# Two 256-token tiles of a unit's first chunks in one PSUM bank, stepped at every second attention item

## Chip, cores and metric

One core of a Trainium2 chip runs the whole kernel. The metric is device time in microseconds (us) of one execution.

## What is computed

Windowed attention with four sink tokens, a dense feed-forward layer with a mish-like gate, and a mixture of four dense experts, each on the output of the one before:

```python
scores = where(is_sink | in_window, q @ k.T / sqrt(D), -1e9)   # B,H,S,D = 2,8,768,64; 4 sinks, window 128
x = softmax(scores) @ v                                        # -> 1536 tokens x 512
h = x @ w_in                                                   # 512 x 2048
x = (h * tanh(log1p(exp(h)))) @ w_out                          # 2048 x 512
p = domain_probs / (domain_probs.sum(-1, keepdims=True) + 1e-9)
out = sum(p[:, e:e+1] * (maximum(x @ w1[e], 0) @ w2[e]) for e in range(4))   # F = 1024
```

## The kernel before

Attention is cut into 24 **items**: for each of two batch entries and three blocks of 256 queries, one item per pair of heads (four pairs). So items 0 to 3 make x for tokens 0 to 255, items 4 to 7 for tokens 256 to 511, items 8 to 15 for tokens 512 to 1023, and items 16 to 23 for the rest. An item computes four score tiles (L231), masks and takes row maxima on VectorE (L234), exponentiates on ScalarE (L238), normalises on GpSimd (L252, L255), transposes on TensorE (L264), multiplies with v (L277, L283), and splits the result into a high and a low part, `xh` (L184) and `xl` (L185, VectorE), since each matrix product of the later layers is three products of such parts (`TERMS`).

The feed-forward layers are cut into **units** of 512 hidden columns: four of the mish layer (unit 0 is the first), then eight of the experts. A unit goes over the tokens in **chunks**, 512 tokens each, except that unit 0 starts with two chunks of 256, because their tokens are ready early. `layer1` makes four hidden tiles (f = 0 to 3) of a chunk, each from 12 matmuls (L477) into one PSUM tile `h`, and then applies `mish`: ScalarE L549 to L552 and L554, VectorE L553, L555 and L556, then the split into `gh` (ScalarE L89) and `gl` (GpSimd L97). L549 is the first to read `h` and L556 the last. `layer2` makes four output tiles (d = 0 to 3) from the four hidden ones, 12 matmuls each (L504) into a PSUM tile `o`, which ScalarE copies to `acc` (L510) in unit 0.

`stream` is a generator that hands out these tiles one **step** at a time: for every chunk, its layer 1 mixed with layer 2 of the chunk before. While attention runs, `banded` takes one step after each item from item 5 on (`LAG`), 19 in all, then nine more that finish the fourth chunk, and `rest` does the other units. The 19 steps are the four of chunk 0, the eight of chunk 1 and seven of the eight of chunk 2; chunk 3 is all in the nine. Beside the steps, `run(w, 1)` converts weights from 64-bit words, after items 0 to 3 and those in `PARK`; this is VectorE's `cv_` work (L117 to L124).

During attention the PSUM pools are small: `x.psum(first, 1, 1)` gives one `h` bank, one `o` bank, and a mish buffer `r` in SBUF. So the 12 matmuls of the next hidden tile can start only when L556 of the tile before has read the bank. After the loop, `first.close()` gives these pools and attention's back, `x.psum(ctx, 3, 3, 2)` makes three `h`, three `o` and two `r` banks in their place, and `x.weights(1)` loads the second unit's weights, parked in DRAM, into SBUF that the closed pools held. The order of every engine's queue comes from a scheduler at compile time: it issues ready instructions by program order, so that steps, items and weight conversion are interleaved.

Of the kernel before, what the change touches and what calls it, by code (L numbers as in the profile page):

```python
# [9 lines left out]
F32 = mybir.dt.float32  # L10
F32R = mybir.dt.float32r
# [6 lines left out]
P = 128  # L18
# [7 lines left out]
QW = 2 * P  # L26
STAGE = 1024
AHEAD = 2
LAG = 5
WARM = 12  # L30
PARK = (8, 10, 12, 14, 16, 18)

class Ctx:
# [3 lines left out]
class Ring:  # L37
# [5 lines left out]
    def next(self):  # L43
        self.n += 1
        return self.tiles[(self.n - 1) % len(self.tiles)]
# [39 lines left out]
def copy(c, eng, out, src):  # L85
    if eng is c.nc.gpsimd:
        eng.tensor_scalar(out, src, 1.0, 0.0, ALU.mult, ALU.add)  # L87
    elif eng is c.nc.scalar:
        eng.activation(out, src, AF.Copy)  # L89
    else:  # L90
        eng.tensor_copy(out, src)


def split(c, hi, lo, src, eng_hi, eng_lo):

    copy(c, eng_hi, hi, src)
    eng_lo.tensor_tensor(lo, src, hi.bitcast(F32), ALU.subtract)  # L97
# [67 lines left out]
def banded_masks(c):  # L165

    nc = c.nc
    rel, sink, diag, prev = c.parts
    m0, m1, m2 = c.masks
    nc.vector.tensor_scalar(sink, sink, c.ns, None, ALU.is_ge)  # L170
    nc.vector.scalar_tensor_tensor(diag, rel, c.win, diag, ALU.is_ge, ALU.add)
    nc.vector.scalar_tensor_tensor(m0[:, 0:P], diag, -BIG, sink, ALU.mult, ALU.mult)
    nc.vector.tensor_scalar(prev, rel, float(P), c.win, ALU.add, ALU.is_ge)
    nc.vector.scalar_tensor_tensor(m1[:, 0:P], prev, -BIG, sink, ALU.mult, ALU.mult)
    for m, at, x in ((m1, P, diag), (m2, 0, prev), (m2, P, sink[:, 0:SINKS]), (m2, SEG, diag)):
        nc.gpsimd.tensor_scalar(m[:, at:at + x.shape[1]], x, -BIG, 0.0, ALU.mult, ALU.add)
# [11 lines left out]
def attention_pools(c, ctx):  # L188
    nc = c.nc
    a = Ctx()  # L190
    a.qk = ctx.enter_context(c.tc.tile_pool(name="a_qk", bufs=4))
    v = c.acc[:, 8:12].rearrange("p a w -> p (a w)")
    a.v = Ring([v[:, 3 * P * n:3 * P * (n + 1)].rearrange("p (n d) -> p n d", n=3) for n in range(5)])
    a.p = ctx.enter_context(c.tc.tile_pool(name="a_p", bufs=3))
    a.st = v[0:4 * SINKS, 15 * P:16 * P]
    a.sm = ctx.enter_context(c.tc.tile_pool(name="a_sm", bufs=3))
    a.ps = ctx.enter_context(c.tc.tile_pool(name="a_ps", bufs=3, space=PSUM))
    a.tr = ctx.enter_context(c.tc.tile_pool(name="a_tr", bufs=2, space=PSUM))
    a.pv = ctx.enter_context(c.tc.tile_pool(name="a_pv", bufs=1, space=PSUM))
    a.vsk = c.vsk  # L200
    return a
# [164 lines left out]
TERMS = ((0, 0), (1, 0), (0, 1))  # L366
# [11 lines left out]
class Experts:  # L378
# [86 lines left out]
    def layer1(self, n, t0, cw, g):  # L465
        c, nc = self.c, self.c.nc
        kind, e, _, _ = self.units[n]
        NF, KT, n1 = self.NF, self.KT, self.n1
        x = (c.xh, c.xl)
        cols = slice(t0, t0 + cw)  # L470
        wis = self.w[n][0]
        for f in range(NF):
            h = self.pa.tile([P, self.CW], F32, tag="h", name="h")[:, 0:cw]
            fs = slice(f * P, (f + 1) * P)
            for k in range(KT):
                for t, (sw, sx) in enumerate(TERMS):
                    nc.tensor.matmul(  # L477
                        h, lhsT=wis[sw][:, k, fs], rhs=x[sx][:, k, cols],
                        start=k == 0 and t == 0, stop=k == KT - 1 and t == 2,
                    )  # L480
            gh = self.gp.tile([P, self.CW], F32R, tag="gh", name="gh")[:, 0:cw]
            gl = self.gp.tile([P, self.CW], F32R, tag="gl", name="gl")[:, 0:cw]
            if kind == 0:
                self.mish(n, gh, gl, h)
            else:
                nc.scalar.activation(gh, h, AF.Relu)  # L486
                nc.vector.scalar_tensor_tensor(gl, h, 0.0, gh.bitcast(F32), ALU.max, ALU.subtract)  # L487
            g.append((gh, gl))
            yield

    def layer2(self, n, t0, cw, g):
        c, nc = self.c, self.c.nc
        kind, e, _, _ = self.units[n]
        NF, KT, n1 = self.NF, self.KT, self.n1
        cols = slice(t0, t0 + cw)
        wos = self.w[n][1]
        if kind == 0:
            accv = self.acc.rearrange("p (ch d) w -> p ch d w", d=KT)
            for d in range(KT):
                o = self.pb.tile([P, cw], F32, tag="o", name="o")  # L500
                ds = slice(d * P, (d + 1) * P)
                for f in range(NF):
                    for t, (sw, sx) in enumerate(TERMS):
                        nc.tensor.matmul(  # L504
                            o, lhsT=wos[sw][:, f, ds], rhs=g[f][sx],
                            start=f == 0 and t == 0, stop=f == NF - 1 and t == 2,
                        )
                y = accv[:, t0 // c.DM, d, t0 % c.DM:t0 % c.DM + cw]
                if n == 0:
                    nc.scalar.activation(y, o, AF.Copy)  # L510
                else:
                    nc.vector.tensor_tensor(y, y, o, ALU.add)
                if n == n1 - 1:
                    split(c, c.xh[:, d, cols], c.xl[:, d, cols], y, nc.scalar, nc.vector)
                yield
            return
        last = n == len(self.units) - 1
        for d in range(cw // P):
            tt = t0 // P + d
            pcol = c.pn[:, tt, e:e + 1]  # L520
            ds = slice(d * P, (d + 1) * P)
            nw = 2 if last and tt == c.T // P - 1 else 1
            for q in range(nw):
                ms = slice(q * c.DM // nw, (q + 1) * c.DM // nw)
                o = self.pb.tile([P, c.DM], F32, tag="o", name="o")[:, ms]
                for f in range(NF):
                    for t, (sw, sx) in enumerate(TERMS):
                        nc.tensor.matmul(  # L528
                            o, lhsT=g[f][sx][:, ds], rhs=wos[sw][:, f, ms],
                            start=f == 0 and t == 0, stop=f == NF - 1 and t == 2,  # L530
                        )
                y = self.acc[:, tt, ms]
                if n == n1:
                    nc.scalar.activation(y, o, AF.Copy, scale=pcol)
                else:
                    nc.vector.scalar_tensor_tensor(y, o, pcol, y, ALU.mult, ALU.add)  # L536
                if last:
                    nc.sync.dma_start(out=c.out[tt * P:(tt + 1) * P, ms], in_=y)
            yield
# [20 lines left out]
def run(gen, n=None):  # L560

    while n is None or n > 0:
        if next(gen, run) is run:
            return
        n = None if n is None else n - 1


def banded(c, ctx, raws):

    tc = c.tc  # L570
    banded_masks(c)
    first = ExitStack()
    x = Experts(c, ctx)
    w = x.weights(0)
    x.psum(first, 1, 1)
    a = attention_pools(c, first)
    steps = x.stream([(0, 0, QW), (0, QW, QW)] + [(0, t0, x.CW) for t0 in range(2 * QW, c.T, x.CW)] + later(c, x, 1))
    dram = ctx.enter_context(tc.tile_pool(name="park", bufs=1, space=bass.MemoryType.DRAM))
    w = chain(w, x.park(dram, 1, "wi"), x.park(dram, 1, "wo"), x.park(dram, 2, "wi"))
    items = c.items  # L580
    raws = dict(enumerate(raws))
    preps = {}
    done = 0
    for m, it in enumerate(items):
        while done <= min(m + AHEAD, len(items) - 1):
            raw = raws.pop(done) if done in raws else load_item(c, *items[done], pool=a.qk)
            preps[done] = raw, attention_values(c, a, *items[done])
            done += 1
        attention_item(c, a, *it, preps.pop(m))
        if m < 4 or m in PARK:  # L590
            run(w, 1)
        if m >= LAG:
            run(steps, 1)
        if m == 0:
            normalize_probs(c)
    first.close()
    x.wpool[1] = ctx.enter_context(tc.tile_pool(name="m_w1", bufs=1))
    x.psum(ctx, 3, 3, 2)
    run(x.weights(1))
    run(steps, 4 * (x.NF + 4) - 4 - (len(items) - LAG))  # L600
    rest(c, x, steps, 1)


# [30 lines left out]
def swa_mish_experts_kernel(ctx: ExitStack, tc: tile.TileContext, qk, v, vsink, n_sink, window, w_in, w_out, probs, w1,  # L634
# [30 lines left out]
    with tc.tile_pool(name="warm", bufs=1, space=PSUM) as wp:  # L665
        o = wp.tile([P, P], F32, name="warm")
        for _ in range(WARM):
            nc.tensor.matmul(o, lhsT=c.ident, rhs=c.ident, start=True, stop=True)
# [73 lines left out]
```

## Time and profile before

| quantity | value |
|---|---|
| runs | 929.54, 937.5, 939.44 us (median 937.5) |
| profiled execution | 931.33 us, of which the profile's span is 929.5 us |
| busy share of the span | TensorE (PE) 97%, its weight loads (PEld) 79%, VectorE (DVE) 46%, ScalarE (ACT) 37%, GpSimd (POOL) 28% |
| mean granted TensorE clock | 0.988 of full speed |
| chain of work that ended last | TensorE 86%, VectorE 10% |

TensorE's busy time counts an instruction from its start to a modelled end, and matmuls overlap; twelve matmuls of 512 columns that are each shown with 0.39 us take 2.72 us together. So in the attention stage a busy share near one does not say that the engine is full; the chain of waits says more.

### The profile page before, as it was taken

Reading aid. Unit: us, or ns where it says so; the run is one execution under the profiler, and the core shown is the slowest. Engines: PE = TensorE matmul, PEld = TensorE weight load, DVE = VectorE, ACT = ScalarE, POOL = GpSimd, SP = SyncE. Lnnn points to the kernel's source line nnn. Section 1 sums busy time; section 2 is a strip of 40 time slices with the busy share of each in tenths; the row PEclk is TensorE's granted clock in tenths of the full one; section 3 lists DMA queues with packets and bytes.
Section 4 is the critical chain, followed back from the end, with each engine's and each line's share of the span. In section 5 each row is a group of like instructions: output and inputs, shape, how many; then the busy total and the mean of one; then the engine's idle time right before and its main releaser. Section 6 shows DMA issues by size and latency. Waiting matters only on the chain.

```text
span 929.5 us, 11138 instructions
## 1 busy us (share of the span) xinstructions
PE 905.6 (97%) x4292; PEld 730.6 (79%) x4292; DVE 424.6 (46%) x770; ACT 347.7 (37%) x745; POOL 263.7 (28%) x217
## 2 busy tenths in 40 slices
PE   6999999799999999999999999999999999999997
PEld 4566767688888888888888888888888888888886
DVE  6999995247698555641112222222222222222222
ACT  4788875487767767722221111111111111111110
POOL 4586663122222434520220220221122112200000
PEclk8999999989999999999999999999999999999999
DMA  7757752062123011001110110110110010000012
GB/s 234 249 189 242 251 215 80 17 255 91 46 90 136 1 46 46 23 23 46 46 40 7 45 46 1 46 46 0 46 46 24 23 45 1 1 1 1 11 46 83
DMA packets 33790, 67.03 MB, mean 72 GB/s; under 512 B 4144, under 2 KB 12592, under 8 KB 33728
## 3 DMA queue, kind: packets, MB, share of 16 engines
q1 hardware_dynamic: 33728, 66.23, 21.1%
q8 instruction: 36, 0.59, 0.3%
q14 instruction: 26, 0.21, 0.1%
HBM read 51.54 MB, written 9.44 MB: 66 GB/s over the span
## 4 chain that ended last, share of the span: by engine, by line
PE 86%; DVE 10%; ACT 1%; DMA 1%; issue 0%; POOL 0%; DVEq 0%; ACTq 0%
PE h L477 42%; PE o L528 28%; PE o L504 14%; DVE pr L234 2%; DVE cv_h L119 1%; DVE cv_a L123 1%; PE pv L277 1%; DVE cv_a L117 1%; DVE cv_r L122 1%; DMA stage<-in_moe_w_in_dram 1%; PE sc L231 1%; PE tp L264 1%; DVE cv_a L121 1%; DVE xl L185 1%; DVE cv_a L118 0%
## 5 line engine op out<-in xcount | busy, mean ns | idle before, releaser
L477 PE MATMUL h<-xh,wih 128*128 128x512 f32 (+1 forms) x592 | 229.2, 387 | 0.3 <-DVE w L556 0.3
L477 PE MATMUL h<-xh,wil 128*128 128x512 f32 (+1 forms) x592 | 227.8, 385 | 0.0
L477 PE MATMUL h<-xl,wih 128*128 128x512 f32 (+1 forms) x592 | 226.8, 385 | 0.0
L486 ACT ACTIVATE gh<-h 128x512 fp32r<-128x512 f32 x96 | 57.4, 598 | 410.1 <-PE h L477 245.2
L487 DVE SCALAR_TENSOR_TENSOR gl<-h,gh 128x512 fp32r<-128x512 f32 x96 | 66.4, 691 | 208.1 <-ACT gh L486 207.9
L528 PE MATMUL o<-wol,gh 128*128 128x512 f32 (+1 forms) x388 | 150.1, 387 | 0.0
L528 PE MATMUL o<-woh,gh 128*128 128x512 f32 (+1 forms) x388 | 150.1, 387 | 0.0
L528 PE MATMUL o<-woh,gl 128*128 128x512 f32 (+1 forms) x388 | 149.9, 387 | 0.0
L536 DVE SCALAR_TENSOR_TENSOR acc<-o,pn,acc 128x512 f32<-128x512 f32 (+1 forms) x85 | 63.3, 745 | 176.2 <-PE o L528 176.2
L477 PEld LDWEIGHTS h<-xh,wih 128*128 128x128 f32 x592 | 111.8, 189 | 24.5 <-DVE cv_a L117 0.7
L477 PEld LDWEIGHTS h<-xl,wih 128*128 128x128 f32 x592 | 111.5, 189 | 22.6 <-issue 0.5
L477 PEld LDWEIGHTS h<-xh,wil 128*128 128x128 f32 x592 | 111.7, 189 | 22.3 <-DVE wil L124 0.3
L97 POOL TENSOR_TENSOR gl<-w,gh 128x512 fp32r<-128x512 f32 (+1 forms) x52 | 68.2, 1312 | 168.0 <-ACT gh L89 167.8
L504 PE MATMUL o<-gh,woh 128*128 128x512 f32 (+1 forms) x208 | 79.4, 382 | 5.4 <-ACT gh L89 5.4
L528 PEld LDWEIGHTS o<-wol,gh 128*128 128x128 f32 x388 | 72.9, 188 | 14.9
L528 PEld LDWEIGHTS o<-woh,gh 128*128 128x128 f32 x388 | 72.9, 188 | 14.9
L528 PEld LDWEIGHTS o<-woh,gl 128*128 128x128 f32 x388 | 72.8, 188 | 14.7
L504 PE MATMUL o<-gh,wol 128*128 128x512 f32 (+1 forms) x208 | 78.2, 376 | 0.0
L504 PE MATMUL o<-gl,woh 128*128 128x512 f32 (+1 forms) x208 | 77.4, 379 | 0.0
L87 POOL TENSOR_SCALAR wih<-stage 128x1024 fp32r<-128x1024 f32 x16 | 16.5, 1048 | 189.4 <-PE h L477 189.4
L553 DVE SCALAR_TENSOR_TENSOR u<-w,r 128x512 f32<-128x512 f32 (+1 forms) x52 | 34.4, 662 | 50.2 <-ACT r L552 49.9
L87 POOL TENSOR_SCALAR woh<-stage 128x1024 fp32r<-128x1024 f32 x16 | 16.5, 1048 | 141.0 <-PE o L528 122.2
(84 smaller groups left out, 1101.5 us busy)
## 6 DMA issues: line engine op xcount, KB each, us to landing
stage<-in_moe_w_dram SPq DMA_DIRECT2D x32, 512.0 KB, 3.7
stage<-in_moe_w_in_dram SPq DMA_DIRECT2D x8, 1024.0 KB, 6.6
stage<-in_moe_w_out_dram SPq DMA_DIRECT2D x8, 1024.0 KB, 5.0
qk<-in_qk_dram SPq DMA_DIRECT2D x16, 324.0 KB, 5.4
acc<-in_v_dram SPq DMA_DIRECT2D x16, 192.0 KB, 3.6
woh<-cv_h SPq DMA_DIRECT2D x6, 512.0 KB, 2.9
out_dram<-acc SPq DMA_DIRECT2D x11, 256.0 KB, 2.0
wih<-cv_h SPq DMA_DIRECT2D x4, 512.0 KB, 3.0
```

Of the source, the lines that this page charges most:

```text
L87: eng.tensor_scalar(out, src, 1.0, 0.0, ALU.mult, ALU.add)
L97: eng_lo.tensor_tensor(lo, src, hi.bitcast(F32), ALU.subtract)
L117: nc.vector.tensor_scalar(af, af, TINY_HI, HUGE_HI, ALU.max, ALU.min)
L119: nc.vector.scalar_tensor_tensor(h, w_hi, -0x40000000, a, ALU.bitwise_and, ALU.bitwise_or)
L234: nc.vector.tensor_tensor_reduce(out=o, in0=sc, in1=c.masks[t if i == 0 else 2][:, 0:sw], scale=-c.scale, scalar=3.0e38, op0=ALU.add, op1= ...
L477: nc.tensor.matmul(h, lhsT=wis[sw][:, k, fs], rhs=x[sx][:, k, cols], start=k == 0 and t == 0, stop=k == KT - 1 and t == 2,)
L486: nc.scalar.activation(gh, h, AF.Relu)
L487: nc.vector.scalar_tensor_tensor(gl, h, 0.0, gh.bitcast(F32), ALU.max, ALU.subtract)
L504: nc.tensor.matmul(o, lhsT=wos[sw][:, f, ds], rhs=g[f][sx], start=f == 0 and t == 0, stop=f == NF - 1 and t == 2,)
L528: nc.tensor.matmul(o, lhsT=g[f][sx][:, ds], rhs=wos[sw][:, f, ms], start=f == 0 and t == 0, stop=f == NF - 1 and t == 2,)
L536: nc.vector.scalar_tensor_tensor(y, o, pcol, y, ALU.mult, ALU.add)
L553: nc.vector.scalar_tensor_tensor(u, w, 1.0, r, ALU.add, ALU.mult)
```

## The change

`mish` and its splits are applied to two hidden tiles at once in the 256-token chunks: the 12 matmuls of tile f write columns 0 to 255 of a bank, those of tile f + 1 columns 256 to 511, and one instruction of 512 columns replaces each two of 256. In `layer2` of these chunks two output tiles share a bank and one copy. Matmuls stay as they are. A step of such a chunk is thus two tiles, and chunk 0 has two steps and chunk 1 four. The items after which a step is taken are listed in `STEPS`: every second one from 5 to 15, and each of 17 to 23. These 13 steps are chunk 0 (5, 7), chunk 1 with layer 2 of chunk 0 (9 to 15), chunk 2 with layer 2 of chunk 1 (17 to 22), and the first hidden tile of chunk 3 (23). Seven steps follow the loop instead of nine.

```diff
-LAG = 5
+STEPS = (5, 7, 9, 11, 13, 15, *range(17, 24))
@@ layer1
-        for f in range(NF):
-            h = self.pa.tile([P, self.CW], F32, tag="h", name="h")[:, 0:cw]
-            fs = slice(f * P, (f + 1) * P)
-            for k in range(KT):
-                for t, (sw, sx) in enumerate(TERMS):
-                    nc.tensor.matmul(
-                        h, lhsT=wis[sw][:, k, fs], rhs=x[sx][:, k, cols],
+        m = self.CW // cw
+        parts = [slice(q * cw, (q + 1) * cw) for q in range(m)]
+        for f0 in range(0, NF, m):
+            h = self.pa.tile([P, self.CW], F32, tag="h", name="h")
+            for f, at in enumerate(parts, f0):
+                fs = slice(f * P, (f + 1) * P)
+                for k in range(KT):
+                    for t, (sw, sx) in enumerate(TERMS):
+                        nc.tensor.matmul(
+                            h[:, at], lhsT=wis[sw][:, k, fs], rhs=x[sx][:, k, cols],
...
-            g.append((gh, gl))
+            g.extend((gh[:, at], gl[:, at]) for at in parts)
@@ layer2
-            for d in range(KT):
-                o = self.pb.tile([P, cw], F32, tag="o", name="o")
+            m = self.CW // cw
+            for d0 in range(0, KT, m):
+                o = self.pb.tile([P, self.CW], F32, tag="o", name="o").rearrange("p (m w) -> p m w", m=m)
+                for d in range(d0, d0 + m):
...
-                y = accv[:, t0 // c.DM, d, t0 % c.DM:t0 % c.DM + cw]
+                ds = slice(d0, d0 + m)
+                y = accv[:, t0 // c.DM, ds, t0 % c.DM:t0 % c.DM + cw]
@@ banded
-        if m >= LAG:
+        if m in STEPS:
             run(steps, 1)
...
-    run(steps, 4 * (x.NF + 4) - 4 - (len(items) - LAG))
+    run(steps, 2 + 4 + 6 + 8 - len(STEPS))
```

## Rows read from the trace of the kernel before

**Rows 1.** Busy us (and instructions) by stretch, then granted clock, DMA share, GB/s

```profile
100.00:125.00 25.00, 24.77 (x174) 17.61 (x174) 24.66 (x59) 20.72 (x66) 15.45 (x17) 1.00 0.75 251
150.00:175.00 25.00, 25.00 (x144) 20.16 (x144) 5.56 (x9) 10.65 (x21) 2.57 (x2) 1.00 0.08 34
175.00:200.00 25.00, 19.65 (x74) 15.63 (x73) 8.26 (x12) 17.61 (x32) 6.24 (x5) 0.86 0.62 228
500.00:600.00 100.00, 100.00 (x443) 82.81 (x442) 26.66 (x37) 11.36 (x19) 20.48 (x12) 1.00 0.10 32
```

**Rows 2.** Chain of waits in time order: start us, length us, engine, tile, line

```profile
94.81 1.07 PE sc L231 x6
...
136.10 1.01 PE sc L231 x2
...
146.29 0.44 PE tp L264 x4
146.73 1.02 PE pv L277 x12
...
149.39 1.43 PE o L504 x12
...
162.77 0.64 PE pv L283 x4
...
202.28 2.72 PE h L477 x12
```

**Rows 3.** Timeline of the tanh that first reads a hidden bank (L549)

```profile
39.44 0.36 ACT L549 ACTIVATE w<-h 128x256 f32<-128x256 f32 x1
...
130.63 0.36 ACT L549 ACTIVATE w<-h 128x256 f32<-128x256 f32 x1
144.21 0.60 ACT L549 ACTIVATE w<-h 128x512 f32<-128x512 f32 x1 [2.21 <-PE h L477]
...
177.49 1.09 ACT L549 ACTIVATE w<-h 128x512 f32<-128x512 f32 x2 [2.49 <-PE h L477]
```

**Rows 4.** Timeline of the items' last instruction (L185): items 0, 15 and 23

```profile
24.25 0.41 DVE L185 TENSOR_TENSOR xl<-pv,xh 128x256 fp32r<-128x256 f32 x1
...
112.99 0.41 DVE L185 TENSOR_TENSOR xl<-pv,xh 128x256 fp32r<-128x256 f32 x1
...
163.86 0.42 DVE L185 TENSOR_TENSOR xl<-pv,xh 128x256 fp32r<-128x256 f32 x1 [0.33 <-ACT xh L184]
```

**Rows 5.** Groups by shape: count, busy us, mean ns, idle before and releasers

```profile
L553 DVE SCALAR_TENSOR_TENSOR u<-w,r 128x512 f32<-128x512 f32 x44 | 30.1, 684 | 50.2 <-ACT r L552 49.9
...
L553 DVE SCALAR_TENSOR_TENSOR u<-w,r 128x256 f32<-128x256 f32 x8 | 4.3, 538 | 0.0
...
L556 DVE SCALAR_TENSOR_TENSOR w<-u,h 128x256 f32<-128x256 f32 x8 | 3.3, 407 | 0.0
```

**Rows 6.** TensorE's timeline around its long wait: start, length, wait before

```profile
178.59 0.84 PE L504 MATMUL o<-gl,woh 128*128 128x512 f32 x3
184.78 0.79 PE L504 MATMUL o<-gh,woh 128*128 128x512 f32 x1 [5.35 <-ACT gh L89]
...
190.92 0.43 PE L477 MATMUL h<-xl,wih 128*128 128x512 f32 x1
```

**Rows 7.** Timeline of VectorE and the DMA queue, and landing time of that DMA

```profile
182.58 0.69 DVE L555 SCALAR_TENSOR_TENSOR u<-u,r 128x512 f32<-128x512 f32 x1 [0.69 <-ACT u L554]
...
183.42 0.34 SPq L434 DMA_DIRECT2D wih<-wi1h  x1
...
wih<-wi1h SPq DMA_DIRECT2D x2, 512.0 KB, 5.6
```

**Rows 8.** Stretches of attention without a step, and where the clock fell

```profile
30.00:37.00 7.00, 5.53 (x35) 3.18 (x34) 7.00 (x21) 4.77 (x15) 2.91 (x4) 1.00 0.67 220
...
66.00:70.00 4.00, 4.00 (x24) 3.46 (x22) 4.00 (x7) 2.34 (x7) 3.80 (x4) 0.74 0.37 121
```

**Rows 9.** The row maxima of the scores by shape, columns as in rows 5

```profile
L234 DVE CUSTOM_DVE_ANT_0 pr<-sc,mask 128x260 f32<-128x260 f32 x64 | 25.3, 415 | 0.3 <-PE sc L231 0.3
```

More of the change, by code (lines that the diff above doesn't have):

```diff
@@ L471, in layer1 @@
         wis = self.w[n][0]
-        for f in range(NF):
-            h = self.pa.tile([P, self.CW], F32, tag="h", name="h")[:, 0:cw]
-            fs = slice(f * P, (f + 1) * P)
-            for k in range(KT):
-                for t, (sw, sx) in enumerate(TERMS):
-                    nc.tensor.matmul(
-                        h, lhsT=wis[sw][:, k, fs], rhs=x[sx][:, k, cols],
[L479 to L482, printed above, removed]
+        m = self.CW // cw
[8 more added lines that the diff above has]
+                            h[:, at], lhsT=wis[sw][:, k, fs], rhs=x[sx][:, k, cols],
+                            start=k == 0 and t == 0, stop=k == KT - 1 and t == 2,
+                        )
+            gh = self.gp.tile([P, self.CW], F32R, tag="gh", name="gh")
+            gl = self.gp.tile([P, self.CW], F32R, tag="gl", name="gl")
             if kind == 0:
@@ L498, in layer2 @@
             accv = self.acc.rearrange("p (ch d) w -> p ch d w", d=KT)
-            for d in range(KT):
-                o = self.pb.tile([P, cw], F32, tag="o", name="o")
[L501 to L507, printed above, removed]
-                y = accv[:, t0 // c.DM, d, t0 % c.DM:t0 % c.DM + cw]
+            m = self.CW // cw
+            for d0 in range(0, KT, m):
+                o = self.pb.tile([P, self.CW], F32, tag="o", name="o").rearrange("p (m w) -> p m w", m=m)
+                for d in range(d0, d0 + m):
+                    ds = slice(d * P, (d + 1) * P)
+                    for f in range(NF):
+                        for t, (sw, sx) in enumerate(TERMS):
+                            nc.tensor.matmul(
+                                o[:, d - d0], lhsT=wos[sw][:, f, ds], rhs=g[f][sx],
+                                start=f == 0 and t == 0, stop=f == NF - 1 and t == 2,
+                            )
+                ds = slice(d0, d0 + m)
+                y = accv[:, t0 // c.DM, ds, t0 % c.DM:t0 % c.DM + cw]
                 if n == 0:
@@ L513, in layer2 @@
                 if n == n1 - 1:
-                    split(c, c.xh[:, d, cols], c.xl[:, d, cols], y, nc.scalar, nc.vector)
+                    split(c, c.xh[:, ds, cols], c.xl[:, ds, cols], y, nc.scalar, nc.vector)
                 yield
```

## The prediction

> **What bounds the kernel now.** I read the busy table by stretch first [rows 1]. From 200 us on TensorE has no gap (443 matmuls in 100 us, 0.226 us each), so a microsecond saved earlier arrives whole at the end, and only the first 200 us can gain. There the stages differ. Up to about 136 us attention runs and VectorE is the full engine: 24.66 of 25 us. From 150 us VectorE is nearly free (5.56 of 25) and TensorE full. In 175 to 200 TensorE is busy 19.65 of 25 and its granted clock is 0.86: something is lost there although nothing bounds the stage.
>
> The chain of waits says where the ownership changes: at 136.10 it passes from VectorE to TensorE for good [rows 2]. Before, VectorE's work sets the pace of the items; after, what counts is how much TensorE has left to do, and whether it can go on without a gap.
>
> Third, the timeline of L549, one per hidden tile [rows 3]. The eight narrow tiles of chunks 0 and 1 start at 39.44 to 130.63 us, (130.63 − 39.44) / 7 = 13.0 us apart, although their 12 matmuls take only some 1.43 us (an `o` tile of that size in [rows 2]). This is the single `h` bank: each tile waits for L556 of the one before, and its eight instructions stand behind attention's and the conversion's on ScalarE and VectorE. So steps handed out at every item (5.9 us, from [rows 4]: (112.99 − 24.25) / 15) are done at every second one, and lag: chunk 2, whose x is complete with item 15 at 113.4 us [rows 4], has its first L549 at 144.21 and its fourth at 177.49 [rows 3].
>
> The lag ends in the stall [rows 6]: TensorE waits 5.35 us until 184.78 for the `gh` of that fourth tile, and then runs at half clock, 1.2 of 2.4 GHz: the 15 matmuls from 184.78 to 190.92 are 6.14 / 14 = 0.44 us apart instead of 0.227 (2.72 / 12, [rows 2]). That is 5.35 + 6.14 − 14 × 0.227 = 8.3 us lost.
>
> **The change, part by part.** *Matmuls.* Number and shape are the same: 0.
>
> *Wide instructions.* Per 256-token pair of tiles, VectorE's three mish instructions are 3 × 0.684 = 2.05 us instead of 2 × 3 × (0.407 to 0.538) = 2.4 to 3.2 [rows 5]; ScalarE's go from 2 × 0.36 to 0.60 each [rows 3]. On their own they would save VectorE 1.6 to 4.7 us over four pairs, but chunk 2 moves into the time in which VectorE sets the pace. By 136 us before, seven narrow tiles have passed VectorE (the eighth's tanh is at 130.63): 7 × 3 × 0.46 = 9.7 us. After, four wide ones and about one and a half of chunk 2: 5.5 × 2.05 = 11.3. VectorE's part of attention thus becomes 1.5 us longer (0 to 3).
>
> *The chain of hidden tiles.* Eight passes through the one bank become four for chunks 0 and 1. A wide pass is not in the trace; it is at least the narrow 13.0 us, and at most that plus 1.43 us of matmuls and eight instructions each 0.28 longer (0.684 − 0.407), 16.7 us. I take 15, as the queues ahead of each instruction stay and most of 13.0 us is queueing. Starts: 41, 56, 71, 86 us, the last done by 101. That is before chunk 2's x at 113.4, which would hold even at 18 us a pass. So chunk 2 follows its data, not the bank: matmuls of its hidden tiles at about 114, 129, 144, and of the fourth near 155 (its passes before were (177.49 − 144.21) / 3 = 11.1 us, [rows 3], mostly beyond attention). The `gh` that TensorE waited for comes at about 163 instead of 184.7.
>
> *What TensorE has left when it takes over.* Before, at 136.10: of chunk 1's layer 2, all but the first output tile's three finished f's cannot have run, as the eighth tile's tanh is at 130.63: 48 − 9 = 39 matmuls of 1.43 / 12 = 0.119 us, 4.6 us; and all of chunk 2's layer 1. After: layer 2 of chunk 1 is done, and two of chunk 2's hidden tiles, 2 × 2.72 = 5.4 us (one to three tiles, 2.7 to 8.2). So 10.1 us go into attention.
>
> Is there room? An item's own matmuls are 4 × 1.07 / 6 + 9 × 0.44 / 4 + 1.02 + 0.64 = 3.4 us of the 5.9 between items [rows 2, 4]. Over the 19 items to 136 us 2.5 × 19 = 47 us are free, and the steps use 8 × 1.43 + 57 × 0.119 = 18 of them, 28 after. The cover suffices on average; but blocks are 24 matmuls (2.86 us) instead of 12 and stand in one queue with the score matmuls that VectorE waits for. Without cover the 10.1 us would come back; I take 2 us as lost (0 to 4), since VectorE waits 0.3 us for scores in the whole trace [rows 9] and has conversion work to fill with.
>
> *Step 13 moves into the loop.* Chunk 3's first hidden tile now uses the old `h` bank and `r`, and item 23 must be complete for it. The second unit's weights, whose SBUF overlaps the closed pools, were asked for at 183.42, right when L555, the last reader of `r`, ended (182.58 + 0.69) [rows 7]. Now: item 23's x at 163.9 + 0.4 [rows 4], up to 2.7 us of matmuls, 182.58 + 0.69 − 177.49 = 5.8 us from L549 to the end of L555, then 5.6 us to land [rows 3, 7]: 176 to 179 us. TensorE's work until then, from 137.6: attention's tail (18 pieces of the chain from 136.10 to 162.77, 12.5 us [rows 2]), two hidden tiles of chunk 2, its layer 2 and chunk 3's layer 1 (5.4 + 10.9 + 10.9): until 177.3. So the wait nearly vanishes: I leave 1.5 us of the 8.3 (0 to 8.3). Eight DMAs of these weights are only earlier; SP's queue issues none between 147.73 and 183.42.
>
> **Sum.** −4.6 − 5.4 (moved) + 1.5 (VectorE) + 2 (blocks) − 8.3 + 1.5 (stall) = −13.3 us. Against the profiled execution, 931.3 − 13.3 = 918. That execution is 6 us below the median of the three runs, 937.5; the four together have a mean of 934.5, and I set the forecast there: 934.5 − 13.3 = **921 us**.
>
> **The rivals.**
> *The stall moves.* If item 23 ends late, or the last wide tile does, the chain old bank → L555 → weights leaves TensorE idle again for the 8.3 us: −13.3 + 6.8 = −6.5, 928 us. For it: the two ends above (177.3 and 176 to 179) are equal within their error. Against it: chunk 3's layer 2 can fill 10.9 us.
> *The lag stays.* If a wide pass takes over 18 us, because its instructions queue behind attention's anyway, chunk 2 is late as before, and only some of layer 2 of chunk 1 moves: −4.6 + 1.5 to nothing, 931 to 935 us.
> *The clock.* Attention without steps between bursts might run at half clock. Attention alone in 30 to 37 us is at 1.00; in 66 to 70 us, with a step, it is 0.74 [rows 8]. The six items from 6 to 16 that now have no step would need 2 × 3.4 − 5.9 = 0.9 us more each, 5 us: 926. The Trainium skill (TensorE: Matmul & The Clock Gate, "HAM oscillation — how this bites in real kernels") says that an engine which pauses between bursts of matmuls is throttled and starts each burst cold; by it, this case would hold. The 1.00 of the stretch without a step speaks against it here.
> *Slower: the blocks hold up the scores.* If each wide step stands in front of score matmuls when VectorE has nothing else, it costs its length: eight double tiles of chunks 0 and 1 (2.86) and three of chunk 2 (2.72), 31 us, less the 15 gained: 950 us. It decides from 25 us of such waits on; before, they are 0.3 us [rows 9].
>
> **How the numbers follow.** The forecast has 0.60 (its own range 911 to 927: everything moved and no loss, 934.5 − 18 = 916, from the lowest run 911; four more lost), the moved stall 0.17, the lag 0.11, the clock 0.04, the slow case 0.08. 909 to 937 leaves out the slow case and 0.1 in all beyond the two ends. About 1% is what a measurement here can tell from no change. Faster by over 1% (under 928): nearly all of the forecast and part of the stall and clock cases, 0.62; the same: the lag and the rest of the stall case, 0.30; slower 0.08.
>
> **What would show it.** Right: wide L549 some 15 us apart from 41 us on, chunk 2's first near 117 and its fourth by 160; no wait of TensorE over 2 us and no fall of the clock between 160 and 200; the weights asked for near 172; the chain passing to TensorE near 138. Wrong: waits of L234 for PE of many us in sum (blocks), a chain owned by VectorE beyond 145 (its work was underrated), a wait of TensorE for weights or `gh` (the stall moved), or L549 over 18 us apart.

## The result and the profile after

The changed kernel takes 947.3 us (median; 946.5 to 949.8), the kernel before 936.3 on the same chip: a ratio of 1.0127 with an interval of 1.0086 to 1.0167. It is 1.3% slower; the forecast was 921. The profiled execution took 946.5 us, its span is 944.7. A few executions of the kernels below ran at a clearly lower granted clock, and ratios and readings leave them out, so that the ratio of such a kernel is below that of the medians.

Lines move a little: L549 to L556 (mish) are now L555 to L562, L477 and L504 (matmuls) are L480 and L509. Busy time by stretch, columns as in [rows 1]:

```profile
100.00:125.00 25.00, 23.82 (x142) 15.53 (x139) 23.00 (x60) 19.14 (x54) 13.80 (x15) 1.00 0.77 255
150.00:175.00 25.00, 23.33 (x131) 16.71 (x129) 10.99 (x23) 13.49 (x32) 12.00 (x12) 0.86 0.13 43
175.00:200.00 25.00, 22.95 (x107) 17.69 (x106) 4.57 (x7) 12.03 (x23) 1.73 (x2) 1.00 0.28 93
```

The loss of 175 to 200 us in [rows 1] (19.65 busy at 0.86) has largely gone. In its place stands one in 150 to 175, where TensorE was full: 23.33 at 0.86. VectorE, nearly always busy at 100 to 125 before (24.66), now idles 2 us there.

The timeline of the tanh that first reads a hidden bank, as in [rows 3], and of the items' last instruction (items 0, 15 and 23), as in [rows 4]:

```profile
43.17 0.58 ACT L555 ACTIVATE w<-h 128x512 f32<-128x512 f32 x1
...
98.94 0.60 ACT L555 ACTIVATE w<-h 128x512 f32<-128x512 f32 x1 [1.66 <-PE h L480]
131.81 0.60 ACT L555 ACTIVATE w<-h 128x512 f32<-128x512 f32 x1
...
176.76 0.60 ACT L555 ACTIVATE w<-h 128x512 f32<-128x512 f32 x1 [2.78 <-PE h L480]
191.25 1.09 ACT L555 ACTIVATE w<-h 128x512 f32<-128x512 f32 x2 [6.60 <-PE h L480]
```

```profile
24.36 0.41 DVE L185 TENSOR_TENSOR xl<-pv,xh 128x256 fp32r<-128x256 f32 x1
...
125.07 0.41 DVE L185 TENSOR_TENSOR xl<-pv,xh 128x256 fp32r<-128x256 f32 x1
...
181.98 0.42 DVE L185 TENSOR_TENSOR xl<-pv,xh 128x256 fp32r<-128x256 f32 x1 [1.42 <-ACT xh L184]
```

The four wide passes are (98.94 − 43.17) / 3 = 18.6 us apart. Items 15 and 23 end 12.1 and 18.1 us later than in [rows 4]. (Where a time is given for an item below, it is the start of this instruction.) And chunk 2's fourth hidden tile is at 176.76 us, where it was at 177.49 [rows 3]: it has hardly moved.

The chain of waits after item 23 (start, length, engine, tile, line; times in us):

```profile
188.21 2.96 PE h L480 x13
...
191.25 1.09 ACT w L555 x2
...
198.03 0.02 SPq L434
198.06 0.03 issue
198.09 0.32 SPq L434
198.41 0.05 issue
198.46 5.87 DMA wil<-wi1l
204.32 0.04 issue
204.37 1.77 PE h L480 x6
```

Here the loss can be read in order. Chunk 3's first hidden tile is complete at 191.2; its last reading of the old `r` (L561) ends at 198.0; only then are the second unit's weights asked for (183.42 in [rows 7]); they land at 204.3. TensorE's timeline names the gaps, the wait ahead of an instruction in brackets:

```profile
199.53 0.50 PE L509 MATMUL o<-gh,woh 128*128 128x512 f32 x1 [1.58 <-ACT gh L89]
203.15 0.47 PE L480 MATMUL h<-xh,wih 128*128 128x512 f32 x1 [1.26 <-DMA wih<-wi1h]
204.37 0.50 PE L480 MATMUL h<-xh,wil 128*128 128x512 f32 x1 [0.74 <-DMA wil<-wi1l]
```

The three gaps come to 3.6 us. The second unit then starts with its hidden tiles late, and its matmuls wait for hidden banks that mish (L562) has not yet read, up to 309 us. One of these waits in the timeline, and all waits ahead of these matmuls in the page (idle time in us, and what ended it); in the kernel before the last number is 0.3:

```profile
283.15 0.50 PE L480 MATMUL h<-xh,wih 128*128 128x512 f32 x1 [1.40 <-DVE w L562]
...
L480 PE MATMUL h<-xh,wih 128*128 128x512 f32 (+1 forms) x592 | 230.7, 390 | 8.4 <-DVE w L562 6.7
```

Over 200 to 420 us, where the kernel before has no gap and 973 matmuls:

```profile
200.00:420.00 220.00, 212.16 (x925) 172.27 (x924) 145.38 (x198) 148.21 (x251) 75.35 (x52) 1.00 0.21 71
```

925 matmuls: 48 × 0.226 = 10.8 us of work that comes later.

### The profile page after: what moved, and what is told of

Read it like the earlier page. It is cut to its first block, busy times and chain, and to the rows that moved or that the text cites. A ratio compares the mean times of both kernels' runs of the same rounds, so it can differ in the third digit from the quotient of the medians.

```text
span 944.7 us, 11089 instructions
## 1 busy us (share of the span) xinstructions
PE 916.5 (97%) x4292; PEld 733.5 (78%) x4292; DVE 426.9 (45%) x758; ACT 346.0 (37%) x717; POOL 261.0 (28%) x213
## 4 chain that ended last, share of the span: by engine, by line
PE 81%; DVE 10%; issue 3%; POOL 2%; DMA 1%; ACT 1%; SPq 0%; DVEq 0%; POOLq 0%; ACTq 0%
PE h L480 38%; PE o L534 28%; PE o L509 9%; PE sc L231 2%; PE pv L277 2%; PE tp L264 1%; DVE pr L234 1%; DVE cv_h L119 1%; DVE cv_a L121 1%; POOL pr L255 1%; POOL gl L97 1%; DVE u L561 1%; DMA stage<-in_moe_w_in_dram 1%; DVE cv_a L123 1%; DVE u L559 1%
## 5 line engine op out<-in xcount | busy, mean ns | idle before, releaser
L480 PE MATMUL h<-xh,wih 128*128 128x512 f32 (+1 forms) x592 | 230.7, 390 | 8.4 <-DVE w L562 6.7
L480 PE MATMUL h<-xh,wil 128*128 128x512 f32 (+1 forms) x592 | 229.1, 387 | 0.7 <-DMA wil<-wi1l 0.7
L480 PE MATMUL h<-xl,wih 128*128 128x512 f32 (+1 forms) x592 | 228.1, 387 | 0.0
L480 PEld LDWEIGHTS h<-xh,wih 128*128 128x128 f32 x592 | 112.4, 190 | 34.8 <-DVE w L562 11.4
L480 PEld LDWEIGHTS h<-xh,wil 128*128 128x128 f32 x592 | 112.5, 190 | 23.5 <-DMA wil<-wi1l 1.3
L480 PEld LDWEIGHTS h<-xl,wih 128*128 128x128 f32 x592 | 112.2, 190 | 23.2 <-issue 1.3
L97 POOL TENSOR_TENSOR gl<-w,gh 128x512 fp32r<-128x512 f32 x48 | 67.9, 1415 | 166.1 <-ACT gh L89 157.5
L534 PEld LDWEIGHTS o<-woh,gh 128*128 128x128 f32 x388 | 72.9, 188 | 14.8
L534 PEld LDWEIGHTS o<-wol,gh 128*128 128x128 f32 x388 | 72.8, 188 | 14.8
L509 PE MATMUL o<-gh,woh 128*128 128x512 f32 (+1 forms) x208 | 78.7, 378 | 2.1 <-ACT gh L89 1.6
L509 PE MATMUL o<-gh,wol 128*128 128x512 f32 (+1 forms) x208 | 77.6, 374 | 0.0
L509 PE MATMUL o<-gl,woh 128*128 128x512 f32 (+1 forms) x208 | 73.0, 376 | 0.0
L559 DVE SCALAR_TENSOR_TENSOR u<-w,r 128x512 f32<-128x512 f32 x48 | 33.6, 701 | 67.3 <-ACT r L558 67.3
L238 ACT ACTIVATE pr<-pr,mx 128x260 f32<-128x260 f32 (+2 forms) x96 | 46.5, 485 | 24.3 <-DVE mx L234 23.0
```

Source lines behind the costliest of these rows:

```text
L238: nc.scalar.activation(o, o, AF.Exp, bias=mx[:, e:e + 1], scale=-1.0, accum_out=sm[:, e:e + 1])
L480: nc.tensor.matmul(h[:, at], lhsT=wis[sw][:, k, fs], rhs=x[sx][:, k, cols], start=k == 0 and t == 0, stop=k == KT - 1 and t == 2,)
L509: nc.tensor.matmul(o[:, d - d0], lhsT=wos[sw][:, f, ds], rhs=g[f][sx], start=f == 0 and t == 0, stop=f == NF - 1 and t == 2,)
L534: nc.tensor.matmul(o, lhsT=g[f][sx][:, ds], rhs=wos[sw][:, f, ms], start=f == 0 and t == 0, stop=f == NF - 1 and t == 2,)
L559: nc.vector.scalar_tensor_tensor(u, w, 1.0, r, ALU.add, ALU.mult)
```

## The experiments

**The step behind item 23.** Is the loss that step, or the sharing? Four kernels answer. The first leaves tiles narrow and takes the new places of the steps (here and below, the number of steps behind the loop changes to match):

```diff
-LAG = 5
+STEPS = (5, 7, 9, 11, 13, 15, *range(17, 24))
@@ layer1 (and layer2 likewise)
+            if (f + 1) % (self.CW // cw) == 0:
                 yield
```

> The kernel before, with the new list of places and two narrow tiles per step there, so that the order of the tiles in the program is that of the changed kernel, but every tile has its own turn in the bank and narrow instructions. If sharing a bank (blocks of 24 matmuls, more of the unit's work inside attention) is what stretched attention: items as in the kernel before (item 15's xl near 113 us, item 23's near 164), first readings of narrow tiles some 13 us apart, total within 1% of before (928 to 945). If the new places did it: item 15 near 125, item 23 near 180, total 945 or more.

946.8 us, 1.0107 (1.0070 to 1.0145): nearly the whole loss without any sharing, and with items 15 and 23 at 117.8 and 169.5 us, so not by late items either. The next has the same edit without item 23, `*range(17, 23)`:

> Narrow tiles at the new places, without the step after item 23. If that step is all that made the narrow kernel at the new places slow: 931 to 937, as the kernel before. If the new places themselves cost: 940 to 947.

936.0 us, 1.0014 (0.9987 to 1.0042). And the changed kernel without its step at item 23, by the same edit:

> The changed kernel without the step after item 23, so that the first hidden tile of the fourth chunk is made after the small pools are closed. If the old bank holds up the tail: attention as in the changed kernel (item 23's xl near 182), but the second unit's weights asked for 5 to 8 us earlier than at 198 us, and 5 to 8 us less in all (938 to 941). If the tail is only late because attention is late: no change, 945 to 949.

934.1 us, 0.9991 (0.9967 to 1.0015): 13.2 us less than with that step, more than the 5 to 8 expected. Third pair: the kernel before, with two more steps behind item 23, its last output tile and this hidden tile.

```diff
-            run(steps, 1)
+            run(steps, 3 if m == 23 else 1)
```

> The kernel before with the last two steps of the changed kernel's list added after item 23: the remaining output tile, and the first hidden tile of the fourth chunk in the old bank. If the old bank and r, held by a tile that needs item 23, cost what the pair of changed kernels shows (13 us): total 945 to 950, the second unit's weights asked for some 8 us or more later than at 183.4 us. If it only cost there because attention was late: 934 to 938.

947.2 us, 1.0132 (1.0085 to 1.0180). So the step costs 11 to 13 us in each pair, with and without sharing, and in the last kernel attention ends early (item 23 at 168.5 us). In each pair it also moves the first request for the second unit's weights by 14 to 17 us. It stands at 198.09 in the changed kernel and at 183.42 in the kernel before [rows 7]; here are, in order, the changed kernel without the step, the narrow one at the new places with it and without it, and the kernel before with it:

```profile
182.98 0.34 SPq L434 DMA_DIRECT2D wih<-wi1h  x1
199.07 0.32 SPq L434 DMA_DIRECT2D wih<-wi1h  x1
185.31 0.34 SPq L434 DMA_DIRECT2D wih<-wi1h  x1
200.72 0.32 SPq L434 DMA_DIRECT2D wih<-wi1h  x1
```

In that last kernel another part of the same chain is the late one. Its TensorE waits:

```profile
188.75 0.79 PE L477 MATMUL h<-xh,wih 128*128 128x512 f32 x1 [3.60 <-DVE w L556]
...
202.15 0.68 PE L504 MATMUL o<-gh,woh 128*128 128x512 f32 x1 [2.57 <-ACT gh L89]
...
206.82 0.50 PE L477 MATMUL h<-xh,wil 128*128 128x512 f32 x1 [0.53 <-DMA wil<-wi1l]
```

Chunk 3's first tile waits for the one `h` bank, which chunk 2's fourth still holds; the weights are asked for at 200.7. Without the step, chunk 3's first tile has a bank of its own, and its tanh runs in one burst with that of the tile before (x2, in the narrow kernel at the new places without item 23):

```profile
179.38 1.09 ACT L551 ACTIVATE w<-h 128x512 f32<-128x512 f32 x2 [2.67 <-PE h L477]
```

**What is left of the change.** Without that step, nothing is gained either. Four kernels tried the likely reasons. Shared bank, but mish for each half (with the step at item 23):

```diff
-                self.mish(n, gh, gl, h)
+                for at in parts:
+                    self.mish(n, gh[:, at], gl[:, at], h[:, at])
```

> The changed kernel, two tiles in one bank, but the mish instructions are narrow again, one set for each half. If the blocks of 24 matmuls in TensorE's queue and the earlier tiles hold attention up: as the changed kernel or 1 to 5 us slower (946 to 952), item 15 at 123 us or later. If the wide instructions on ScalarE, VectorE and GpSimd do it: item 15 near 115, total 935 to 941.

965.4 us, 1.0300 (1.0249 to 1.0352), 18 us over the changed kernel and beyond both forecasts: without the wide instructions a shared bank costs much. A bank is handed on only when both halves are through, which would explain it; no run takes that apart. Fewer steps in the loop, `STEPS = (5, 7, 9, 11, 13, 15)`:

> The changed kernel with only the six double steps after items 5 to 15 inside attention; the third chunk and all behind it come after the small pools are closed. If attention is stretched by the amount of the unit's work inside it: item 15 near 125 us as in the changed kernel, then the items of the second half at the pace of the kernel before (6.4 us each), item 23 near 170; the work left out comes after it, total 930 to 942. If it is stretched by the shared bank's blocks alone: item 23 near 180 only if the loss is all ahead of item 15, and the same 930 to 942 in total. No gap of TensorE over 2 us and the weights asked for by 172 in either, since no chain of the third chunk stands in the old bank.

936.9 us, 1.0012 (0.9981 to 1.0044): no late wait of TensorE, but a granted clock of 0.80 to 0.91 in stretches of 100 to 160 us. Attention's items put ahead in the compile-time order (on the kernel without item 23):

```diff
-        attention_item(c, a, *it, preps.pop(m))
+        with tc.high_priority(offset=600):
+            attention_item(c, a, *it, preps.pop(m))
```

> The changed kernel without the step after item 23, where the scheduler ranks an item's instructions some 600 places ahead of the steps around it (about four items' worth), so that blocks of the steps stand behind attention in the queues when both are ready. If blocks ahead of score and transpose matmuls stretch attention: item 23's xl back to 165 to 170 us from 181.6, total 922 to 930. If attention is stretched by something else (wide instructions already in a queue, the clock): item 23 still near 180, total 930 to 940; if the steps then come too late, TensorE has a gap behind attention.

940.6 us, 1.0048 (1.0017 to 1.0079): items 15 and 23 are later still (134.0 and 192.2, in a profiled execution of 944.2 us). And the kernel before without steps in the loop (`LAG = 24`):

> The kernel before with no step inside attention: all of the first unit's tiles after item 23. It prices what the steps cost attention. If TensorE is full in attention and each microsecond of step work inside it comes back as later items: item 23's xl near 140 us, total within 1% of before (930 to 945). If attention has room for steps, as the prediction had it (18 of 47 us free): item 23 still beyond 155, total 18 us or more above before (953 or more).

961.2 us, 1.0121 (1.0054 to 1.0187). By the ratio, all 19 steps that the kernel before takes in the loop are worth some 0.012 × 935.5 = 11 us together, 5 to 17 by the interval; the one step behind item 23 loses as much.

**A balance.** To see where a kernel loses time, take for each stretch its length minus busy time × granted clock: about what TensorE could have done and did not (busy time has modelled ends, so it is not exact). Two stretches decide. In order: the kernel before; narrow at the new places without item 23; the changed kernel without item 23; and two that come below, the kernel before stopped at item 19 and at item 17 (the same two stretches of each, and one more of the last):

```profile
150.00:165.00 15.00, 15.00 (x94) 11.79 (x94) 3.49 (x6) 6.62 (x14) 1.86 (x2) 1.00 0.14 56
...
180.00:200.00 20.00, 15.22 (x54) 12.29 (x55) 8.26 (x12) 15.10 (x28) 4.96 (x4) 0.83 0.77 284
```

```profile
150.00:165.00 15.00, 15.00 (x96) 12.38 (x94) 3.89 (x8) 7.56 (x17) 1.28 (x1) 1.00 0.21 71
...
180.00:200.00 20.00, 14.65 (x59) 11.63 (x58) 8.26 (x12) 16.34 (x31) 4.40 (x4) 0.91 0.66 242
```

```profile
150.00:165.00 15.00, 13.35 (x69) 9.57 (x68) 7.79 (x18) 8.73 (x24) 10.44 (x11) 0.77 0.21 70
...
180.00:200.00 20.00, 19.53 (x91) 16.02 (x89) 8.81 (x14) 16.39 (x30) 4.33 (x4) 1.00 0.75 258
```

```profile
150.00:165.00 15.00, 15.00 (x91) 11.93 (x89) 6.95 (x9) 5.86 (x12) 3.97 (x4) 1.00 0.21 70
...
180.00:200.00 20.00, 20.00 (x90) 16.57 (x89) 9.62 (x14) 16.50 (x31) 5.17 (x4) 1.00 0.58 222
```

```profile
135.00:150.00 15.00, 12.50 (x85) 8.45 (x82) 14.88 (x32) 11.36 (x33) 9.01 (x12) 0.88 0.46 170
150.00:165.00 15.00, 15.00 (x66) 11.79 (x66) 6.45 (x8) 5.52 (x13) 4.10 (x3) 0.78 0.21 70
...
180.00:200.00 20.00, 20.00 (x96) 16.77 (x95) 8.47 (x13) 16.35 (x30) 5.17 (x4) 1.00 0.44 156
```

For the kernel before, 180 to 200 us lose 20 − 15.22 × 0.83 = 7.4; for the changed one without item 23, 150 to 165 us lose 15 − 13.35 × 0.77 = 4.7. Worked out likewise for the other stretches (us lost, one profiled execution each):

| kernel | 15–40 | 40–135 | 135–165 | 165–200 | 200–420 | profiled time | time less losses |
|---|---|---|---|---|---|---|---|
| before | 7.1 | 5.3 | 2.3 | 7.9 | 0.0 | 931.3 | 908.7 |
| narrow, new places, no 23 | 10.5 | 6.2 | 1.3 | 6.7 | 0.0 | 931.7 | 907.1 |
| before, stop at 19 | 11.9 | 7.7 | 2.5 | 0.7 | 0.0 | 931.0 | 908.2 |
| before, stop at 17 | 11.7 | 9.0 | 7.3 | 0.6 | 0.0 | 936.6 | 908.1 |
| changed | 10.3 | 6.0 | 5.1 | 2.1 | 7.8 | 946.5 | 915.2 |
| changed, no 23 | 10.2 | 6.0 | 5.1 | 0.5 | 0.0 | 933.4 | 911.6 |
| wide layer 1 alone, no 23 | 11.5 | 7.1 | 1.1 | 0.2 | 2.9 | 934.5 | 911.7 |
| wide layer 2 alone, no 23 | 11.9 | 7.9 | 5.7 | 7.7 | 0.0 | 942.4 | 909.2 |

If the balance closed, the last column would be one number. It is 907 to 912 us, and 915 for the changed kernel with its many waits, so a difference of a few us in it can't be placed. It does not go with sharing alone: four other kernels with layer 1 shared (six steps, both kernels of halves below, mish for each half) have 909.3 to 909.8, and the kernel before with the step at item 23 has 911.4. So the change without its last step does remove the loss behind the loop (6.7 to 0.5), and pays 3.8 us of it in the last items of attention; where the rest goes stays open. The first column would explain why this profile of the kernel before lies low among its runs (929 to 940 us): its granted clock was 0.86 in 15 to 40 us, where these others have 0.56 to 0.66.

**Why the items are late.** First the blocks of 24 matmuls: shared bank, but each step cut in two, one per item (a `yield` between the halves, steps at items 5 to 22, two at 5 and 7).

> The shared bank, the wide activations and evictions, and the same work inside the attention loop as the wide kernel without the step at item 23; but each step is cut in two, so that twelve matmuls (one tile of 256 tokens) are issued per item from item 5 to item 22, with two tiles at items 5 and 7 alone. If the blocks of 24 matmuls stretch the attention loop (theory): the pace of items 3 to 15 and 15 to 23 returns to that of the narrow kernels (76 and 51 us), item 23 stands at 165 to 169 us, no TensorE wait of microseconds follows, and the time is 923 to 930 us. If it is the wide instructions, or the work that has moved into the loop, that stretches it (rival): item 23 stands at 178 us or later and the time is 932 to 936 us, as in the wide kernel without the step.

933.3 us, 0.9971 (0.9951 to 0.9992), item 23 at 181.3: the rival was right, the length of a block is not it. Then the same halves at the places of the kernel before, items 5 to 23:

> The shared bank and the wide activations and evictions, with one tile of 256 tokens at each item from 5 to 23, as in the kernel before: nothing but the sharing differs from it. If blocks stretch the loop (theory): item 23 stands at 162 to 167 us, the wait of some 5 us for the old bank's gh after item 23 and the time of the kernel before return (933 to 938 us). If the wide instructions stretch the loop (rival): the first pass ends later, item 15 stands at 120 us or later, and the time is 940 us or more.

935.6 us, 1.0009 (0.9977 to 1.0041); item 15 at 128.6, item 23 at 189.9, against 113.0 and 163.9 [rows 4] with the same work handed out at the same items. So the sharing itself delays the items, though not the time. How far is less sure: some 3 us are the lower early clock, and the profiled execution took 941.8 us, 6 above the median, with a clock of 0.56 in 150 to 165 us. One thing that differs is the order that the compiler writes into TensorE's queue: ahead of the last score matmul stand 6.0 hidden and 4.0 output tiles (in tiles of 512 columns) in the changed kernel and in these two, 4.0 and 2.4 in the kernel before. Which of the two sharings does it? Layer 2 alone shared, then layer 1 alone, the other narrow with two tiles per step, both without item 23:

> Output tiles (layer 2) share a bank and one eviction; hidden tiles stay narrow, two per step, at the new places without item 23. The compiled order on TensorE has 4.0 hidden and 2.4 output tiles ahead of the last score matmul, as in the kernel before. If unit work ordered ahead of the last scores makes the items late (theory): item 23 ends at 165 to 170 us, the wait for the old bank's gh after it stays, and the time is 933 to 938 us. If the shared output bank with its 256-wide blocks and wide eviction is what delays items (rival): item 23 ends after 175 us.

942.6 us, 1.0064 (1.0042 to 1.0086), item 23 at 179.6, the wait for `gh` still 5.4 us. The theory is wrong here: its order is that of the kernel before, and the items are late all the same. So are those of the kernel with six steps, which has 4.0 and 2.0 tiles there and item 23 at 177.8.

> Hidden tiles (layer 1) share a bank, the activations and the products; output tiles stay narrow, two per step, at the new places without item 23. The compiled order on TensorE has 6.0 hidden and 4.0 output tiles ahead of the last score matmul, as in the wide kernel. If that order makes the items late (theory): item 23 ends at 178 to 184 us, the wait after the loop is gone, and the time is 931 to 936 us. If it is the shared output bank (rival): item 23 ends before 172 us.

935.1 us, 0.9975 (0.9954 to 0.9996), item 23 at 175.8, no wait behind the loop. Neither sharing explains it alone: each delays the items by 8 to 12 us against 167.3 in the narrow kernel, and layer 1's is the one that ends the wait. In the chain of waits of the changed kernel GpSimd has 14.8 us of 40 to 190 us, against 0.2 before. A part of it, ahead of a fall of the clock:

```profile
148.82 1.12 POOL sk L244
150.00 2.95 POOL pr L255 x2
153.03 1.06 POOL sm L239
154.09 0.11 issue
154.20 1.06 PE tp L264 x8
...
159.26 4.33 PE h L480 x12
```

The 12 matmuls from 159.26 take 0.36 us each instead of 0.227 [rows 2]. Does GpSimd, which now also makes a `gl` of 512 columns at a time, hold the items? Two kernels on the changed one without item 23, which has the same 14.8 us, move or halve it:

```diff
-        split(c, gh, gl, w, nc.scalar, nc.gpsimd)
+        split(c, gh, gl, w, nc.scalar, nc.vector if n == 0 else nc.gpsimd)
```

> The wide kernel without the step at item 23, with the subtraction that makes gl of the first unit on VectorE instead of GpSimd. If the wide gl on GpSimd, standing ahead of attention's normalisation, makes the items late (theory): GpSimd's share of the chain in 40 to 190 us falls from 14.8 to under 5 us, item 23 ends before 175 us instead of 181.6, and the time is 926 to 931 us. If it does not (rival): VectorE only has some 0.7 us more for each of eight tiles, item 23 stays at 180 us or later, and the time is 934 us or more.

933.0 us, 0.9974 (0.9953 to 0.9995), between the two forecasts: GpSimd leaves the chain entirely and item 23 is at 177.2, 4.4 us earlier, but the loss in 135 to 165 us grows to 8.1 (clock 0.81 and 0.74). So GpSimd holds up the items at most in part; with it out of the way other waits take its place, such as 5.3 us for a DMA of converted weights (`wi2l`) at 132 us in this kernel's chain, and the time hardly changes.

> The wide kernel without the step at item 23, with gl of the first unit on GpSimd in two instructions of 256 columns. If one long GpSimd instruction is what holds attention (theory): item 23 ends 3 us or more before 181.6, and the time is 928 to 933 us. If the queue's order and not the length of one instruction decides (rival): item 23 within 3 us of 181.6 and the time 933 to 937 us.

935.4 us, 0.9999 (0.9979 to 1.0019), item 23 at 182.4: as the rival said. What sets the late items is not settled beyond this: they come with the sharing of either layer; the order ahead of the scores is not it alone, nor the length of a block or of a `gl`.

**Where to stop.** If the loss behind the loop comes from an old-bank tile that is in its mish when the loop ends, the narrow kernel should gain by ending its steps earlier:

```diff
-        if m >= LAG:
+        if LAG <= m < 20:
```

> The kernel before with its steps at items 5 to 19 alone: the third chunk's tiles from its fourth on (and the last tiles of the second chunk's layer 2) are issued after the loop, in the new banks. If the 8.3 us that TensorE loses after item 23 in the kernel before come from the old bank's handover (theory): the wait and the half clock behind it are gone, and the time is 926 to 930 us. If the work taken out of items 20 to 23 only follows later at the same cost, with TensorE at a lower clock while items 20 to 23 run alone (rival): TensorE's clock falls under 0.9 in the 25 us ahead of item 23, and the time stays at 933 to 938 us.

930.3 us, 0.9931 (0.9905 to 0.9957): the wait has gone, and this kernel beats both. Its chunk 2 has only two tiles in the old bank; the other tiles run in the new ones. With `m < 22`:

> The kernel before with its steps at items 5 to 21 alone. If every old-bank tile that is still in its mish when the loop ends costs its handover (theory): the fourth hidden tile of the third chunk is out of the loop, the wait of 5.35 us is gone, and the time is between the one that stops at 19 (930.3 us) and 934 us. If the gain needs two free items or more at the end (rival): the wait stays at 3 us or more, and the time is 935 us or more.

934.6 us, 0.9983 (0.9959 to 1.0006): a wait of 4.0 us for `gh` stays, so the theory missed; a third tile in the old bank is one too many. With `m < 18`:

> The kernel before with its steps at items 5 to 17 alone (15 was the last of the second chunk's own; 16 and 17 start the third chunk). If the gain of stopping at item 19 came from having no old-bank tile in its mish when the loop ends (theory): the wait after the loop is gone here too, and the time is 926 to 933 us. If TensorE lacks work in the last items (rival): its clock is under 0.9 in 140 to 170 us, and the time is 934 us or more.

934.7 us, 0.9973 (0.9944 to 1.0001): no wait, but now only one hidden tile is left for the last items (item 17's step; item 16's is still chunk 1's), the clock is 0.88 and 0.78 in 135 to 165 us, and 7.3 us are lost there, against 2.5: the rival. Last, the halves of the shared bank, stopped at item 19 too:

> The shared bank with one tile of 256 tokens per item, at items 5 to 19 alone: what stopping at item 19 does to the narrow kernel, with sharing. The compiled order has 6.0 hidden and 3.0 output tiles ahead of the last score matmul. If that order costs what the missing wait saves (theory): item 23 ends at 172 us or later, and the time is 930 to 936 us, not below the narrow kernel that stops there (930.3 us). If sharing saves work that shows once the end of the loop is free of old-bank tiles (rival): 922 to 928 us.

935.7 us, 0.9993 (0.9970 to 1.0015), item 23 at 178.9: sharing takes back the gain of stopping.

## Why the prediction was wrong

Forecast and result lie 26 us apart. Half is the step at item 23; the other half is the forecast gain of 13.3 us, which does not come even without that step (934.1 us).

*"Step 13 moves into the loop"* is the step that failed with the loss. It left 1.5 us of a stall (0 to 8.3) and had the second unit's weights land at 176 to 179 us; the step costs 11 to 13 us, and they land at 204.3. Its terms: item 23's x at 182.4 instead of 164.3 (18.1 late); 8.8 us instead of 2.7 until the tile's last matmul at 191.2, since the bank comes free only at 184.0, when L562 of chunk 2's fourth tile ends, and the queue then holds layer 2's matmuls first; 6.8 instead of 5.8 for the mish; 6.2 instead of 5.6 to land. Together 25.9 us. The rival "the stall moves" named this very chain, old bank to L555 to weights, but at 6.8 us and a chance of 0.17; the price was one stall, while the pairs show 11 to 13 us. It should have been priced as what it is: one more pass through a single bank, put between the end of the loop and the weights, with the waits for hidden tiles that follow in the second unit. And the two narrow kernels with this step show that lateness of attention was not even needed: the bank held by chunk 2's fourth tile does the same (3.60 us of waiting above).

*The chain of hidden tiles.* A wide pass was put at 15 us, with 16.7 as its end; it is 18.6. The bound took the queueing of a narrow pass as fixed, yet a step at every second item brings the items' own pace in: (125.07 − 39.11) / 12 = 7.2 us per item (item 3 ends at 39.11), so 14.3 between steps before any wait. Chunk 2's passes are (176.76 − 131.81) / 3 = 15.0 us, not 11.1. Thus the condition of "the lag stays", a pass over 18 us, came true: the fourth tile is at 176.8, not 160. That the kernel without the step then lies in that rival's 931 to 935 us is in part luck, since more work moved than it had.

*The stall.* It goes, as forecast, but for a reason that gains nothing. The fourth tile's `gh` is not earlier (its L89 starts at 184.01 us, before at 184.10); TensorE still has attention's own matmuls at 180 us, so it is not yet where it used to wait.

*Moved work.* Its size was right: 3.6 tiles more ahead of the last scores, 3.6 × 2.72 = 9.8 us against 10.1. That it would be a gain assumed free room in attention, and the working had too much of it: it took four score matmuls per item, where the trace of the kernel before has eight (192 of L231 in 24 items). An item's own matmuls are then 4.1 us, not 3.4, and some 35 us were free, not 47, for steps of 28 us. By the balance, TensorE loses more in 40 to 165 us than in the narrow kernel at the same places: 11.1 us against 7.5.

*VectorE and blocks*, +1.5 and +2. The row maxima of the scores, as in [rows 9]:

```profile
L234 DVE CUSTOM_DVE_ANT_0 pr<-sc,mask 128x260 f32<-128x260 f32 x64 | 25.5, 416 | 4.4 <-PE sc L231 4.4
```

4.4 us of waiting for scores instead of 0.3: above the 0 to 4 given for the blocks, far from the 25 at which that rival decides. But with the blocks cut in two the waits for scores are 4.2 us, so the length of a block was not their cause. VectorE's own 1.5 us were not measured apart.

*The clock* had 0.04. Among the items that lost their step it did not do what the rival had: 40 to 135 us have 0.98 before and after. It fell later, among items that have one: TensorE waits 1.06 us at 154.2 and 0.56 us at 155.8, and has 0.77 in 150 to 165 us, partly at its lower level of 1.2 GHz. The one stretch at 1.00 in [rows 8], held against that rival, was too short to speak for it; in the profile after, the same 30 to 37 us have 0.80.

The Trainium skill (TensorE: Matmul & The Clock Gate, "HAM oscillation — how this bites in real kernels") describes that an engine whose bursts of matmuls are parted by waits falls to half clock and starts the next burst cold. The rows of 150 to 165 us agree (0.77), and so does the kernel stopped at item 17 (0.78).

*The base* was sound: 934.5 against medians of 934.4 to 936.6 for the kernel before.

## What to carry to other kernels

When a stage's buffers are closed and their space goes to the next stage's weights, the last user of the old buffers starts that load: put no work with a long tail there, and price such a move as a whole pass, its waits, its products, the landing and the waits behind it, not as the wait seen so far. A wait that vanishes is only a gain if the thing waited for came earlier; if the waiting engine came later, the time has moved, and length minus busy time × clock, summed over stretches, shows roughly where to. The work filled in beside a stage has a best amount: here two hidden tiles of 512 columns in the last items gain 0.7%, with three or four the wait is there, and with one the clock falls.

## What the runs showed of the hardware

The last items of attention, with one hidden tile beside them, ran at a granted clock of 0.88 and 0.78 (135 to 150 and 150 to 165 us of the kernel stopped at item 17), with two at 0.89 and 1.00 (stopped at item 19). In the changed kernel without item 23, six `gl` of 512 columns run on GpSimd in 40 to 165 us: the first two took 2.23 and 2.27 us, the other four 1.27 to 1.45, against 1.41 on average over the whole kernel; what stretched the two was not tried. And the clock of 15 to 40 us, ahead of nearly all steps, was 0.86 in one profile and 0.56 to 0.66 in the others, worth 3 to 5 us; what sets it was not tried.
